# Another order for the opening of a one-core sum of linear attention and a gated product: loads, value projections and first half units

## The chip, the cores and the metric

The kernel runs on one core of a Trainium2 chip. The metric is the device time of one execution in microseconds (us); the median of several executions counts. TensorE (PE) multiplies 128x128 weights with a moving operand and writes to PSUM, of which there are eight banks. ScalarE (ACT) and VectorE (DVE) copy and combine what lies there; GpSimd (POOL) works on SBUF; SyncE (SP) issues the loads.

## The reference, cut to what matters

```python
x = A_x                                   # 1 x 2048 x 512, bf16
xn = _layernorm(x, axis=-1)
# A: linear attention, 32 heads of 16
qkv = (xn @ wqkv)...                      # q, k, v
pq, pk = einsum(q, w_phi), einsum(k, w_phi)
phi = concatenate([softmax(p), softmax(-p)])      # for q and for k
kv = einsum("bhsf,bhsd->bhfd", phi_k, v); z = sum of phi_k over s
o = einsum(phi_q, kv) / (einsum(phi_q, z) + 1e-6)
# B: gated bilinear
g = einsum("bsd,df->bsf", xn, w_gate); u = einsum("bsd,df->bsf", xn, w_up)
return x + o @ wo + (g * u) @ w_down      # F = 1792
```

## The kernel before

The 2048 tokens are 16 tiles (NT) of 128, in groups of four (GT). A tile is normalised with tokens on the partitions (xn, 128x512); the products need it transposed, features on the partitions (xnT, four chunks of 128). For tiles 0 to 3 the transposes are made on TensorE with an identity (lt, line 216): four 128x128 transposes write one PSUM bank (tp), and ScalarE copies it to xnT in two halves of 128x256 (line 223, parts=2). Later tiles are normalised on ScalarE and transposed by DMA (ln_block).

The order of each engine's instructions is the order in which the code issues them (a manual schedule): no planner moves them. Each engine does its own in that order and waits at semaphores, which the build sets by what writes and reads each tile. So the code from line 378 on, the opening, is the schedule:

- first_stats, first_std, first_apply: mean and variance of a tile on VectorE (ln_sums, line 161), the root on ScalarE (line 371), reciprocal and scaling on VectorE (lines 375 and 177).
- warm_up (line 324): matmuls of ones into a bank that nobody reads, nine at the start and one after the transposes of tile 0.
- vproj(n) (line 332 on): the values of tile n, four matmuls of 128x512 (proj, line 252), evicted to vt on ScalarE or VectorE (line 339). For tile 0 the transposes of tile 1 stand between its first two matmuls and the last two, and its eviction is issued later.
- unit(T, f, lo, hi): for a group T of four tiles and a chunk f of 128 hidden features, four gate matmuls and four up matmuls (line 288), the gate copied by ScalarE (g_sb, line 294) and multiplied with up by VectorE (hT, line 297). For f = 0 and 1 of group 0 it is done in halves of 256 tokens, tiles 0 and 1 first; the transposes of tile 2 and 3 stand between gate and up of these half units (amid), and the copies of tile 2 and 3 after the gate's copy.
- then the values of tiles 2 and 3, the table load for exp, the second halves (unit(0, f, 2 * P, TT)), and from there whole units in turn with the folding of w_phi into the k weights (fold, line 243), kproj, kv and so on.

All PSUM tiles but kv come from one pool of six banks in rotation (bank); the two others are kvps, opened ahead of the opening, which accumulate phi_k with v later.

SP's queue has the loads in this order: x of tiles 0 and 1, the two halves of wv, x of tiles 2 and 3, gate and up weights of chunks 0 and 1 (dma_gu, line 78), wphi, gate and up of chunks 2 and 3, and so on.

Of the kernel before, what the change touches and what calls it, by code (L numbers as in the profile page):

```python
# [8 lines left out]
BF16 = mybir.dt.bfloat16  # L9
F32 = mybir.dt.float32  # L10
AF = mybir.ActivationFunctionType
ALU = mybir.AluOpType
# [9 lines left out]
def kernel(  # L22
# [51 lines left out]
    def dma_x(lo, hi):  # L74
        nc.sync.dma_start(out=xall[:, lo:hi, :], in_=x_view(lo, hi))  # L75
# [4 lines left out]
    def dma_gu(lo, hi):  # L80
        dma_cols(nc.sync, wg, B_w_gate, lo * P, hi * P)
        dma_cols(nc.sync, wu, B_w_up, lo * P, hi * P)
# [3 lines left out]
    for lo in (0, 2):  # L86
        nc.sync.dma_start(out=wv[:, lo:lo + 2, :],  # L87
                          in_=A_wqkv[lo * P:(lo + 2) * P, 2 * D:3 * D].rearrange("(c p) f -> p c f", p=P))
    dma_x(2, 3)
    dma_x(3, 4)  # L90
    dma_gu(0, 2)
    nc.sync.dma_start(out=wphi[:], in_=A_w_phi.rearrange("(c h) d f -> (h d) c f", c=DC))
    dma_gu(2, 4)
    nc.sync.dma_start(out=wT2[:, 1, :, :], in_=A_wqkv[:, D:2 * D], transpose=True)
# [59 lines left out]
    def bank(name, dt=F32, n=TT):  # L154
        return ps_s.tile([P, n], dt, name=name, tag="s")
# [3 lines left out]
    def ln_sums(n):  # L159
        stats = lnpool.tile([P, nc.vector.BN_STATS_DIM], F32, name="stats")  # L160
        nc.vector.bn_stats(out=stats[:], in_=xall[:, n, :])  # L161
        return stats
# [12 lines left out]
    def ln_apply(n, mean, rstd):  # L175
        xn = xnpool.tile([P, D], BF16, name="xn")
        nc.vector.tensor_scalar(out=xn[:], in0=xall[:, n, :], scalar1=mean, scalar2=rstd,
                                op0=ALU.subtract, op1=ALU.mult)
        xns[n] = xn

    def mv_tile():
        return lnpool.tile([P, GT, nc.vector.BN_AGGR_DIM], F32, name="mv", bufs=GT)
# [30 lines left out]
        for i in range(GT):  # L213
            chores.append(lambda i=i: apply(i))

    def lt(n, parts=1, later=False):
        tp = bank("tp", BF16).rearrange("p (c t) -> p c t", c=DC)
        for c in range(DC):
            nc.tensor.transpose(out=tp[:, c, :], in_=xns[n][:, c * P:(c + 1) * P], identity=ident[:])

        def copies():
            for c in range(0, DC, DC // parts):
                nc.scalar.copy(out=xnT[:, c:c + DC // parts, n * P:(n + 1) * P], in_=tp[:, c:c + DC // parts, :])  # L223

        if later:
            return copies
        copies()

    bd = consts.tile([P, DC, 8, DH], BF16)

# [19 lines left out]
    def proj(ps, n, w, js=range(DC)):  # L250
        for j in js:
            nc.tensor.matmul(ps, lhsT=xnT[:, j, n * P:(n + 1) * P], rhs=w[:, j, :],  # L252
                             start=(j == 0), stop=(j == DC - 1))
# [24 lines left out]
    hTs = {}  # L278
    units = [(T, f) for T in range(NGRP) for f in range(FC)]

    def unit(T, f, lo=0, hi=TT, amid=None):
        if T not in hTs:
            hTs[T] = hpool.tile([P, FC, TT], BF16, name="hT", tag="h")
        pss = []
        for w, name in ((wg, "g"), (wu, "u")):
            ps = bank(name)[:, 0:hi - lo]
            for c in range(DC):
                nc.tensor.matmul(ps, lhsT=w[:, c, f * P:(f + 1) * P], rhs=xnT[:, c, T * TT + lo:T * TT + hi],  # L288
                                 start=(c == 0), stop=(c == DC - 1))
            pss.append(ps)  # L290
            if amid is not None and name == "g":
                copies = amid()
        g_sb = gpool.tile([P, TT], BF16, name="g_sb")
        nc.scalar.copy(out=g_sb[:, 0:hi - lo], in_=pss[0])  # L294
        if amid is not None:
            copies()
        nc.vector.tensor_tensor(out=hTs[T][:, f, lo:hi], in0=pss[1], in1=g_sb[:, 0:hi - lo], op=ALU.mult)  # L297

    def ffn(k):
        for _ in range(k):  # L300
# [24 lines left out]

    warm_up(9)

    with tc.tile_pool(name="ps_k", bufs=1, space=PSUM) as ps_k:
        kvps = [ps_k.tile([P, 4, 4, E1], F32, name=f"kv{b}") for b in range(2)]
        phiks = {}  # L330

        def vproj(n, copy=nc.scalar.copy, amid=None, later=False):
            ps = bank("pv")
            proj(ps, n, wv, range(2))
            if amid is not None:
                amid()
            proj(ps, n, wv, range(2, DC))
            def evict():
                copy(out=vts[n % NV][:, :, :, 0:DH], in_=ps.rearrange("p (a b c) -> p a b c", a=8, b=4))
            if later:  # L340
                return evict
            evict()

        def kproj(n, pf=None):
            phiks[n] = features(n, W1k, "k", pf)

        def vkproj(n):
            pv, pk = bank("pv"), bank("k")
            for j in range(DC):
                proj(pv, n, wv, (j,))  # L350
                proj(pk, n, W1k, (j,))
            nc.scalar.copy(out=vts[n % NV][:, :, :, 0:DH], in_=pv.rearrange("p (a b c) -> p a b c", a=8, b=4))  # L352
            kproj(n, pk)

        def kv(n):
            vt, phik = vts[n % NV], phiks[n]
            for gr in range(NG):
                nc.tensor.matmul(kvps[gr // 4][:, gr % 4, :, :].rearrange("p a b -> p (a b)"),  # L358
                                 lhsT=phik[:, gr, :], rhs=vt[:, gr, :, :].rearrange("p a b -> p (a b)"),
                                 start=(n == 0 and gr % 4 == 0), stop=(n == NT - 1 and gr % 4 == 3))  # L360

        mvs = [mv_tile() for n in range(GT)]
        stds = {}

        def first_stats(n):
            stats = ln_sums(n)
            nc.vector.bn_aggr(out=mvs[n][:, 0, :], in_=stats[:])

        def first_std(n):
            stds[n] = lnpool.tile([P, 1], F32, name="std", bufs=GT)  # L370
            nc.scalar.activation(out=stds[n][:], in_=mvs[n][:, 0, 1:2], func=AF.Sqrt, bias=epst[:], scale=1.0)

        def first_apply(n):
            rstd = lnpool.tile([P, 1], F32, name="rs1", bufs=GT)
            nc.vector.reciprocal(out=rstd[:], in_=stds[n][:])
            ln_apply(n, mvs[n][:, 0, 0:1], rstd[:])

        first_stats(0)
        first_std(0)
        stats1 = ln_sums(1)  # L380
        first_apply(0)
        nc.vector.bn_aggr(out=mvs[1][:, 0, :], in_=stats1[:])
        first_std(1)
        first_apply(1)
        first_stats(2)
        stats3 = ln_sums(3)
        lt(0, parts=2)
        warm_up(1)
        copy_v = vproj(0, amid=lambda: lt(1, parts=2), later=True)
        first_std(2)  # L390
        first_apply(2)
        copy_v()
        nc.vector.bn_aggr(out=mvs[3][:, 0, :], in_=stats3[:])
        first_std(3)
        first_apply(3)
        make_bd()
        nc.gpsimd.tensor_tensor(out=M4[:], in0=BO[:, 0:4, :], in1=BO[:, 4:8, :], op=ALU.add)
        vproj(1)
        unit(0, 0, 0, 2 * P, amid=lambda: lt(2, parts=2, later=True))
        unit(0, 1, 0, 2 * P, amid=lambda: lt(3, parts=2, later=True))  # L400
        vproj(2, copy=nc.vector.tensor_copy)
        vproj(3, copy=nc.vector.tensor_copy)
        table(AF.Exp, 1)
        for f in range(2):
            unit(0, f, 2 * P, TT)
        del units[0:2]
        ffn(1)
        for j0 in (0, 2):
            fold(1, W1k, j0, (nc.scalar.copy, nc.vector.tensor_copy))
        ffn(1)  # L410
        ln_block(4)
        ffn(1)
        chore(2)
        kproj(0)
        ffn(1)
        chore(2)
        ffn(1)
        chore()
        kproj(1)
        ffn(1)  # L420
        chore()
        ffn(1)
        kproj(2)
        chore()
        ffn(1)
        kv(0)
        chore()
        ffn(1)
        kproj(3)
        chore()  # L430
        ffn(1)
        kv(1)
        nc.sync.dma_start(out=wT2[:, 0, :, :], in_=A_wqkv[:, 0:D], transpose=True)
        for n in range(GT, NT):
            if n in (4, 8):
                ln_block(n + 4)
            vkproj(n)
            chore(1 if n % GT < 2 else 0)
            ffn(1)
            kv(n - 2)  # L440
            chore((1, 2, 2, 2)[n % GT])
            if n >= 8 and n % 2 == 0:
                qproj((n - 8) // 2)
            if n == 6:
                fold(0, W1q, 0)
            ffn(1)
            if n == 6:
                fold(0, W1q, 2)
        ffn(1)
        kv(NT - 2)  # L450
        ffn(1)
        kv(NT - 1)
        for b in range(2):
            nc.vector.tensor_tensor(out=KV[:, 4 * b:4 * b + 4, :, :], in0=kvps[b][:],
                                    in1=_bcast_ap(M4[:], [M4[:].ap[0], [0, 4], [E1, 4], [1, E1]]), op=ALU.mult)
        qproj(4)
        ffn(1)
# [64 lines left out]
```

## Time and profile before

| | |
|---|---|
| Time, three executions | 222.0, 222.24, 222.48 us; median 222.24 |
| Profiled execution | 222.45 us; span of its instructions 220.7 us |
| TensorE's last matmul ends | 217.89 us after the span's start |
| Matmuls in the span | 1284 recorded |

Times in the profile count from the span's start. A row of the timeline merges neighbours of one line on one engine: start, time from the first's start to the last's end, engine, line, operation, what is written and read, and how many. A matmul's duration contains its way through the array, so neighbours overlap; the distance of their starts is what TensorE spends on each. The square brackets give the idle time of the engine before, and what ended it. PEld is the loading of the weights, which overlaps the matmul before it. When the loads land, in us: x of tile 0 at 2.80, of tile 1 at 3.35, wv at 4.58 and 5.33, x of tile 2 at 6.08, of tile 3 at 6.72, gate weights of chunks 0 and 1 at 8.35, up weights of these at 9.32, wphi at 9.58.

The opening on VectorE, for tiles 2 and 3:

```profile
6.11 0.69 DVE L161 BATCH_NORM_STATS2 stats<-xall 128x6 f32<-128x512 bf16 x1 [0.22 <-DMA xall<-in_A_x_dram]
8.05 0.16 DVE L375 RECIPROCAL rs<-std 128x1 f32<-128x1 f32 x1 [0.45 <-ACT std L371]
8.25 0.41 DVE L177 TENSOR_SCALAR xn<-xall,mv,rs 128x512 bf16<-128x512 bf16 x1
9.12 0.16 DVE L375 RECIPROCAL rs<-std 128x1 f32<-128x1 f32 x1 [0.36 <-ACT std L371]
```

### The profile page before, as it was taken

The numbers are of one execution on the slowest core, as the hardware profiler recorded it, in microseconds if no ns is written. First come the engines' busy times: TensorE is split into PE (matmuls) and PEld (weight loads), VectorE is DVE, ScalarE is ACT, GpSimd is POOL, SyncE is SP. The second block draws the span as 40 slices with busy tenths as digits, with TensorE's granted clock in tenths as the row PEclk, the third lists the DMA queues.
The fourth block names the chain that finished last, engine by engine and source line by source line (L and its number), as shares of the span: only waits on it lengthen the run. The fifth ranks groups of instructions, "written<-read, shape, count | busy, mean of one in ns | idle before, by whom it ended". The sixth has DMA issues, their size and how long they took to land.

```text
span 220.7 us, 3490 instructions
## 1 busy us (share of the span) xinstructions
PE 215.6 (98%) x1284; PEld 104.8 (47%) x1308; DVE 138.7 (63%) x241; ACT 89.5 (41%) x170; POOL 68.8 (31%) x54
## 2 busy tenths in 40 slices
PE   8999999999999999999999999999999999999994
PEld 2554444445444444444544444444444444454443
DVE  4657985785569685757589964197645745454321
ACT  3755575449764875545353221231322323100000
POOL 3000455545335653637333643033033033000000
PEclk9999999999999999999999999999999999999999
DMA  5999983503200324020206645214431431422401
GB/s 182 237 310 386 367 217 69 97 0 48 31 18 12 57 43 81 9 42 1 49 1 96 119 97 109 62 24 95 95 74 24 95 71 28 91 52 71 71 27 48
DMA packets 47249, 19.91 MB, mean 90 GB/s; under 512 B 37504, under 2 KB 46976, under 8 KB 47104
## 3 DMA queue, kind: packets, MB, share of 16 engines
q1 hardware_dynamic: 47232, 19.69, 38.2%
q8 instruction: 10, 0.16, 0.3%
q14 instruction: 7, 0.06, 0.1%
HBM read 8.67 MB, written 2.10 MB: 49 GB/s over the span
## 4 chain that ended last, share of the span: by engine, by line
PE 94%; DMA 2%; SPq 1%; issue 1%; ACT 0%; DVE 0%
PE u L288 22%; PE fin L310 22%; PE g L288 21%; PE fin L313 6%; PE k L252 6%; PE q L252 6%; PE pv L252 5%; DMA wu<-in_B_w_up_dram 2%; PE ab L465 2%; PE kv L358 2%; SPq L75 1%; PE pq L243 1%; SPq L87 0%; SPq L78 0%; ACT g_sb L294 0%
## 5 line engine op out<-in xcount | busy, mean ns | idle before, releaser
L288 PE MATMUL u<-xnT,wu 128*128 128x512 bf16 (+1 forms) x229 | 57.7, 372 | 0.4
L288 PE MATMUL g<-xnT,wg 128*128 128x512 bf16 (+1 forms) x222 | 56.7, 372 | 0.4
L297 DVE TENSOR_TENSOR hT<-u,g_sb 128x512 bf16<-128x512 f32 (+1 forms) x58 | 37.3, 649 | 26.3 <-PE u L288 16.9
L265 DVE TENSOR_REDUCE sums<-e 128x64 f32<-128x1024 f32 x32 | 38.9, 1216 | 21.8 <-ACT e L262 21.8
L294 ACT CAST g_sb<-g 128x512 bf16<-128x512 f32 (+1 forms) x58 | 33.4, 576 | 45.9 <-PE g L288 45.7
L310 PE MATMUL fin<-wd,hT 128*128 128x512 bf16 (+2 forms) x234 | 50.9, 366 | 0.3
L269 POOL TENSOR_TENSOR phiq<-e,rs 128x1024 bf16<-128x1024 f32 x16 | 30.9, 1932 | 60.8 <-DVE rs L267 53.6
L269 POOL TENSOR_TENSOR phik<-e,rs 128x1024 bf16<-128x1024 f32 x16 | 30.9, 1932 | 55.5 <-DVE rs L267 44.0
L288 PEld LDWEIGHTS <-wu 128*128 128x128 bf16 x232 | 22.6, 98 | 25.8 <-DMA wu<-in_B_w_up_dram 0.2
L310 PEld LDWEIGHTS <-hT 128*128 128x128 bf16 x238 | 22.4, 98 | 24.7
L288 PEld LDWEIGHTS <-wg 128*128 128x128 bf16 x232 | 21.9, 98 | 23.4 <-DMA wg<-in_B_w_gate_dram 0.2
L252 PEld LDWEIGHTS <-xnT 128*128 128x128 bf16 x192 | 17.4, 98 | 18.7 <-ACT xnT L223 1.3
L316 DVE TENSOR_TENSOR o_sb<-fin,xall 128x512 bf16<-128x512 f32 (+2 forms) x17 | 11.2, 657 | 22.3 <-PE fin L313 22.2
L252 PE MATMUL pv<-wv,xnT 128*128 128x512 bf16 x62 | 22.1, 386 | 0.1
L252 PE MATMUL k<-W1k,xnT 128*128 128x512 bf16 x63 | 21.9, 379 | 0.1
L261 ACT ACTIVATE e<-q 128x512 f32<-128x512 f32 x16 | 9.5, 596 | 25.4 <-PE q L252 20.0
L267 DVE RECIPROCAL rs<-sums 128x64 f32<-128x64 f32 x32 | 17.7, 553 | 3.1
L313 PE MATMUL fin<-wo,oT 128*128 128x512 bf16 (+2 forms) x68 | 16.6, 367 | 0.0
L252 PE MATMUL q<-W1q,xnT 128*128 128x512 bf16 x60 | 15.9, 378 | 0.1
L352 ACT CAST vt<-pv 128x512 bf16<-128x512 f32 x12 | 7.0, 587 | 17.4 <-PE pv L252 17.4
L161 DVE BATCH_NORM_STATS2 stats<-xall 128x6 f32<-128x512 bf16 x16 | 10.7, 667 | 1.4 <-DMA xall<-in_A_x_dram 1.4
L474 DVE TENSOR_TENSOR otok<-ab,rden 128x512 bf16<-128x512 f32 x16 | 11.1, 691 | 0.6
(51 smaller groups left out, 118.6 us busy)
## 6 DMA issues: line engine op xcount, KB each, us to landing
out_dram<-o_sb SPq DMA_DIRECT2D x15, 128.0 KB, 2.0
wd<-in_B_w_down_dram SPq DMA_DIRECT2D x1, 1792.0 KB, 15.9
wg<-in_B_w_gate_dram SPq DMA_DIRECT2D x2, 640.0 KB, 6.8
wu<-in_B_w_up_dram SPq DMA_DIRECT2D x2, 640.0 KB, 8.0
xall<-in_A_x_dram SPq DMA_DIRECT2D x1, 1024.0 KB, 11.9
xall<-in_A_x_dram SPq DMA_DIRECT2D x4, 128.0 KB, 2.7
wv<-in_A_wqkv_dram SPq DMA_DIRECT2D x2, 256.0 KB, 3.0
wg<-in_B_w_gate_dram SPq DMA_DIRECT2D x2, 256.0 KB, 4.8
```

The lines of the kernel that those rows point to most:

```text
L161: nc.vector.bn_stats(out=stats[:], in_=xall[:, n, :])
L252: nc.tensor.matmul(ps, lhsT=xnT[:, j, n * P:(n + 1) * P], rhs=w[:, j, :], start=(j == 0), stop=(j == DC - 1))
L265: nc.vector.tensor_reduce(out=sums[:], in_=ev, axis=AX.X, op=ALU.add)
L267: nc.vector.reciprocal(out=rs[:].rearrange("p a b -> p (a b)"), in_=sums[:])
L269: nc.gpsimd.tensor_tensor(out=phi[:].rearrange("p g (x f) -> p (g x) f", f=DH), in0=ev, in1=rs[:].to_broadcast((P, 2 * H, DH)), op=ALU.mult)
L288: nc.tensor.matmul(ps, lhsT=w[:, c, f * P:(f + 1) * P], rhs=xnT[:, c, T * TT + lo:T * TT + hi], start=(c == 0), stop=(c == DC - 1))
L294: nc.scalar.copy(out=g_sb[:, 0:hi - lo], in_=pss[0])
L297: nc.vector.tensor_tensor(out=hTs[T][:, f, lo:hi], in0=pss[1], in1=g_sb[:, 0:hi - lo], op=ALU.mult)
L310: nc.tensor.matmul(ps, lhsT=hTs[T][:, f, t4 * P:(t4 + 1) * P], rhs=wd[:, f, lo:lo + w], start=(f == 0), stop=False)
L313: nc.tensor.matmul(ps, lhsT=oTs[n][:, c, :], rhs=wo[:, c, lo:lo + w], start=False, stop=(c == DC - 1))
L316: nc.vector.tensor_tensor(out=o_sb[:], in0=ps, in1=xall[:, n, lo:lo + w], op=ALU.add)
L474: nc.vector.tensor_tensor(out=o_tok[:].rearrange("p (b h d) -> p b h d", b=2, d=DH), in0=abv[:, :, :, 0:DH], in1=rden[:].to_broadcast((P, ...
```

## The change

Two loads change places: the gate weights of chunks 0 and 1 come before x of tile 3, the up weights after it. lt now issues two transposes, the copy of these, two transposes, the copy of these; in the built program the third transpose of each tile carries a wait for that first copy. unit is split into half (four matmuls), gate_copy and hidden, which the opening calls one by one. The opening has a new order: after the values of tiles 0 and 1 come the gate of half unit 0, the transposes of tile 2, the gate of half unit 1, the values of tile 2, both ups, the transposes of tile 3 and its values. The values of tiles 0 and 1 lie in two PSUM banks of their own (ps_v), which are given back before kvps takes them. Statistics of tiles 2 and 3 are taken one after the other, each with its scaling; make_bd moves to the opening's end; the copies of the values are a function of their own (vcopy). What follows the table load is as before.

```diff
--- before.py
+++ after.py
@@ -87,8 +87,9 @@
         nc.sync.dma_start(out=wv[:, lo:lo + 2, :],
                           in_=A_wqkv[lo * P:(lo + 2) * P, 2 * D:3 * D].rearrange("(c p) f -> p c f", p=P))
     dma_x(2, 3)
+    dma_cols(nc.sync, wg, B_w_gate, 0, 2 * P)
     dma_x(3, 4)
-    dma_gu(0, 2)
+    dma_cols(nc.sync, wu, B_w_up, 0, 2 * P)
     nc.sync.dma_start(out=wphi[:], in_=A_w_phi.rearrange("(c h) d f -> (h d) c f", c=DC))
     dma_gu(2, 4)
     nc.sync.dma_start(out=wT2[:, 1, :, :], in_=A_wqkv[:, D:2 * D], transpose=True)
@@ -213,18 +214,13 @@
         for i in range(GT):
             chores.append(lambda i=i: apply(i))
 
-    def lt(n, parts=1, later=False):
+    def lt(n, parts=2):
         tp = bank("tp", BF16).rearrange("p (c t) -> p c t", c=DC)
-        for c in range(DC):
-            nc.tensor.transpose(out=tp[:, c, :], in_=xns[n][:, c * P:(c + 1) * P], identity=ident[:])
-
-        def copies():
-            for c in range(0, DC, DC // parts):
-                nc.scalar.copy(out=xnT[:, c:c + DC // parts, n * P:(n + 1) * P], in_=tp[:, c:c + DC // parts, :])
-
-        if later:
-            return copies
-        copies()
+        step = DC // parts
+        for lo in range(0, DC, step):
+            for c in range(lo, lo + step):
+                nc.tensor.transpose(out=tp[:, c, :], in_=xns[n][:, c * P:(c + 1) * P], identity=ident[:])
+            nc.scalar.copy(out=xnT[:, lo:lo + step, n * P:(n + 1) * P], in_=tp[:, lo:lo + step, :])
 
     bd = consts.tile([P, DC, 8, DH], BF16)
 
@@ -278,23 +274,27 @@
     hTs = {}
     units = [(T, f) for T in range(NGRP) for f in range(FC)]
 
-    def unit(T, f, lo=0, hi=TT, amid=None):
+    def half(w, name, T, f, lo, hi):
+        ps = bank(name)[:, 0:hi - lo]
+        for c in range(DC):
+            nc.tensor.matmul(ps, lhsT=w[:, c, f * P:(f + 1) * P], rhs=xnT[:, c, T * TT + lo:T * TT + hi],
+                             start=(c == 0), stop=(c == DC - 1))
+        return ps
+
+    def gate_copy(ps, n):
+        g_sb = gpool.tile([P, TT], BF16, name="g_sb")
+        nc.scalar.copy(out=g_sb[:, 0:n], in_=ps)
+        return g_sb
+
+    def hidden(T, f, ps, g_sb, lo, hi):
         if T not in hTs:
             hTs[T] = hpool.tile([P, FC, TT], BF16, name="hT", tag="h")
-        pss = []
-        for w, name in ((wg, "g"), (wu, "u")):
-            ps = bank(name)[:, 0:hi - lo]
-            for c in range(DC):
-                nc.tensor.matmul(ps, lhsT=w[:, c, f * P:(f + 1) * P], rhs=xnT[:, c, T * TT + lo:T * TT + hi],
-                                 start=(c == 0), stop=(c == DC - 1))
-            pss.append(ps)
-            if amid is not None and name == "g":
-                copies = amid()
-        g_sb = gpool.tile([P, TT], BF16, name="g_sb")
-        nc.scalar.copy(out=g_sb[:, 0:hi - lo], in_=pss[0])
-        if amid is not None:
-            copies()
-        nc.vector.tensor_tensor(out=hTs[T][:, f, lo:hi], in0=pss[1], in1=g_sb[:, 0:hi - lo], op=ALU.mult)
+        nc.vector.tensor_tensor(out=hTs[T][:, f, lo:hi], in0=ps, in1=g_sb[:, 0:hi - lo], op=ALU.mult)
+
+    def unit(T, f, lo=0, hi=TT):
+        pg = half(wg, "g", T, f, lo, hi)
+        pu = half(wu, "u", T, f, lo, hi)
+        hidden(T, f, pu, gate_copy(pg, hi - lo), lo, hi)
 
     def ffn(k):
         for _ in range(k):
@@ -325,21 +325,65 @@
 
     warm_up(9)
 
+    def vcopy(n, ps, copy=nc.scalar.copy):
+        copy(out=vts[n % NV][:, :, :, 0:DH], in_=ps.rearrange("p (a b c) -> p a b c", a=8, b=4))
+
+    mvs = [mv_tile() for n in range(GT)]
+    stds = {}
+
+    def first_std(n, stats):
+        nc.vector.bn_aggr(out=mvs[n][:, 0, :], in_=stats[:])
+        stds[n] = lnpool.tile([P, 1], F32, name="std", bufs=GT)
+        nc.scalar.activation(out=stds[n][:], in_=mvs[n][:, 0, 1:2], func=AF.Sqrt, bias=epst[:], scale=1.0)
+
+    def first_apply(n):
+        rstd = lnpool.tile([P, 1], F32, name="rs1", bufs=GT)
+        nc.vector.reciprocal(out=rstd[:], in_=stds[n][:])
+        ln_apply(n, mvs[n][:, 0, 0:1], rstd[:])
+
+    with tc.tile_pool(name="ps_v", bufs=1, space=PSUM) as ps_v:
+        pv = [ps_v.tile([P, D], F32, name=f"pv{n}") for n in range(2)]
+        first_std(0, ln_sums(0))
+        stats = ln_sums(1)
+        first_apply(0)
+        first_std(1, stats)
+        first_apply(1)
+        lt(0)
+        warm_up(1)
+        proj(pv[0][:], 0, wv, range(2))
+        lt(1)
+        proj(pv[0][:], 0, wv, range(2, DC))
+        proj(pv[1][:], 1, wv)
+        first_std(2, ln_sums(2))
+        first_apply(2)
+        vcopy(0, pv[0])
+        g = [half(wg, "g", 0, 0, 0, 2 * P)]
+        lt(2)
+        g.append(half(wg, "g", 0, 1, 0, 2 * P))
+        pv2 = bank("pv")
+        proj(pv2, 2, wv)
+        stats = ln_sums(3)
+        g_sb = [gate_copy(g[0], 2 * P)]
+        first_std(3, stats)
+        first_apply(3)
+        g_sb.append(gate_copy(g[1], 2 * P))
+        vcopy(1, pv[1])
+        u0 = half(wu, "u", 0, 0, 0, 2 * P)
+        hidden(0, 0, u0, g_sb[0], 0, 2 * P)
+        vcopy(2, pv2, nc.vector.tensor_copy)
+        u1 = half(wu, "u", 0, 1, 0, 2 * P)
+        hidden(0, 1, u1, g_sb[1], 0, 2 * P)
+        lt(3)
+        pv3 = bank("pv")
+        proj(pv3, 3, wv)
+        make_bd()
+        vcopy(3, pv3, nc.vector.tensor_copy)
+        table(AF.Exp, 1)
+        nc.gpsimd.tensor_tensor(out=M4[:], in0=BO[:, 0:4, :], in1=BO[:, 4:8, :], op=ALU.add)
+
     with tc.tile_pool(name="ps_k", bufs=1, space=PSUM) as ps_k:
         kvps = [ps_k.tile([P, 4, 4, E1], F32, name=f"kv{b}") for b in range(2)]
         phiks = {}
-
-        def vproj(n, copy=nc.scalar.copy, amid=None, later=False):
-            ps = bank("pv")
-            proj(ps, n, wv, range(2))
-            if amid is not None:
-                amid()
-            proj(ps, n, wv, range(2, DC))
-            def evict():
-                copy(out=vts[n % NV][:, :, :, 0:DH], in_=ps.rearrange("p (a b c) -> p a b c", a=8, b=4))
-            if later:
-                return evict
-            evict()
 
         def kproj(n, pf=None):
             phiks[n] = features(n, W1k, "k", pf)
@@ -349,7 +393,7 @@
             for j in range(DC):
                 proj(pv, n, wv, (j,))
                 proj(pk, n, W1k, (j,))
-            nc.scalar.copy(out=vts[n % NV][:, :, :, 0:DH], in_=pv.rearrange("p (a b c) -> p a b c", a=8, b=4))
+            vcopy(n, pv)
             kproj(n, pk)
 
         def kv(n):
@@ -359,48 +403,6 @@
                                  lhsT=phik[:, gr, :], rhs=vt[:, gr, :, :].rearrange("p a b -> p (a b)"),
                                  start=(n == 0 and gr % 4 == 0), stop=(n == NT - 1 and gr % 4 == 3))
 
-        mvs = [mv_tile() for n in range(GT)]
-        stds = {}
-
-        def first_stats(n):
-            stats = ln_sums(n)
-            nc.vector.bn_aggr(out=mvs[n][:, 0, :], in_=stats[:])
-
-        def first_std(n):
-            stds[n] = lnpool.tile([P, 1], F32, name="std", bufs=GT)
-            nc.scalar.activation(out=stds[n][:], in_=mvs[n][:, 0, 1:2], func=AF.Sqrt, bias=epst[:], scale=1.0)
-
-        def first_apply(n):
-            rstd = lnpool.tile([P, 1], F32, name="rs1", bufs=GT)
-            nc.vector.reciprocal(out=rstd[:], in_=stds[n][:])
-            ln_apply(n, mvs[n][:, 0, 0:1], rstd[:])
-
-        first_stats(0)
-        first_std(0)
-        stats1 = ln_sums(1)
-        first_apply(0)
-        nc.vector.bn_aggr(out=mvs[1][:, 0, :], in_=stats1[:])
-        first_std(1)
-        first_apply(1)
-        first_stats(2)
-        stats3 = ln_sums(3)
-        lt(0, parts=2)
-        warm_up(1)
-        copy_v = vproj(0, amid=lambda: lt(1, parts=2), later=True)
-        first_std(2)
-        first_apply(2)
-        copy_v()
-        nc.vector.bn_aggr(out=mvs[3][:, 0, :], in_=stats3[:])
-        first_std(3)
-        first_apply(3)
-        make_bd()
-        nc.gpsimd.tensor_tensor(out=M4[:], in0=BO[:, 0:4, :], in1=BO[:, 4:8, :], op=ALU.add)
-        vproj(1)
-        unit(0, 0, 0, 2 * P, amid=lambda: lt(2, parts=2, later=True))
-        unit(0, 1, 0, 2 * P, amid=lambda: lt(3, parts=2, later=True))
-        vproj(2, copy=nc.vector.tensor_copy)
-        vproj(3, copy=nc.vector.tensor_copy)
-        table(AF.Exp, 1)
         for f in range(2):
             unit(0, f, 2 * P, TT)
         del units[0:2]
```

## The prediction

> **What bounds the kernel now.** I read the page first. TensorE is busy over nearly the whole span, and the chain of work that ended last is TensorE's matmuls:
>
> ```profile
> PE 215.6 (98%) x1284; PEld 104.8 (47%) x1308; DVE 138.7 (63%) x241; ACT 89.5 (41%) x170; POOL 68.8 (31%) x54
> PE 94%; DMA 2%; SPq 1%; issue 1%; ACT 0%; DVE 0%
> ```
>
> So a microsecond that TensorE loses or wins anywhere in its stream moves the end by as much, unless it waits later for something timed by a DMA. The busy times of the stretches say that it hardly does: from 12.6 us on TensorE (the first figure after the stretch's length) is busy 204.09 of 208.10 us, of which 2.8 us lie after its last matmul (217.89 us), and the view of waits shows in that stretch no weight load that waits for a DMA.
>
> ```profile
> 12.60:220.70 208.10, 204.09 (x1228) 99.31 (x1249) 131.10 (x215) 81.78 (x152) 66.96 (x44) 1.00 0.36 83
> ```
>
> The change lies before 12.6 us. So the third view is TensorE's timeline there (start, duration, line, how many). Tile n's four transposes are a tp row:
>
> ```profile
> 4.88 0.61 PE L219 MATMUL tp<-ident,xn 128*128 128x128 bf16 x4
> 5.28 0.63 PE L324 MATMUL warm<-const-bfloat16-1.0 128*128 128x512 bf16 x1
> 5.95 0.97 PE L252 MATMUL pv<-wv,xnT 128*128 128x512 bf16 x2
> 6.75 0.39 PE L219 MATMUL tp<-ident,xn 128*128 128x128 bf16 x4
> 6.98 1.66 PE L252 MATMUL pv<-wv,xnT 128*128 128x512 bf16 x6
> 8.48 0.60 PE L288 MATMUL g<-xnT,wg 128*128 128x256 bf16 x4
> 8.92 0.39 PE L219 MATMUL tp<-ident,xn 128*128 128x128 bf16 x4
> 9.37 0.61 PE L288 MATMUL u<-xnT,wu 128*128 128x256 bf16 x4
> 11.13 1.67 PE L252 MATMUL pv<-wv,xnT 128*128 128x512 bf16 x7
> ```
>
> and the waits, with ScalarE's copies of the transposes:
>
> ```profile
> PEld L252 <- ACT xnT L223: 1.3, 3, 0.6
> PEld L288 <- DMA wu<-in_B_w_up_dram: 0.2, 1, 0.2
> ```
>
> ```profile
> 5.52 0.65 ACT L223 COPY xnT<-tp 128x256 bf16<-128x256 bf16 x2 [0.28 <-PE tp L219]
> 7.18 0.65 ACT L223 COPY xnT<-tp 128x256 bf16<-128x256 bf16 x2 [1.01 <-PE tp L219]
> ```
>
> What to see. In single instructions the four transposes of tile 1 start at 6.75, 6.81, 6.87 and 6.92, the first copy of them at 7.18, its release comes at 7.56, and the matmul that needs it starts at 7.605: **0.683 us from a transpose's start, over ScalarE, back to TensorE** (0.256 + 0.381 + 0.046). For tile 0 it is 5.17 to 5.95, 0.778, as TensorE runs at half pace: 128x512 matmuls follow one another by 0.427 us until 6.7 and by 0.216 after (the granted clock reads 1.00 throughout, since its record begins at 6.72; the pitch tells more). TensorE's idle time here is 0.245 ahead of pv at 5.95 and 0.195 ahead of 7.605 (both for that copy), and 0.23 ahead of 9.37 (up weights, landed 9.32): 0.67 in all, and the change can win no more than that.
>
> **The change part by part.** TensorE does the same 16 transposes, 16 v matmuls and 16 half-width gate and up matmuls; only order and waits differ.
>
> *Transposes in two halves.* This decides. Before, four transposes of a tile ran, then two copies. Now it is two, copy, two, copy, into one PSUM bank, and in the built program the third transpose of each tile carries a wait for the copy of the first two. TensorE takes matmuls in order, so everything behind waits too. Price, by the hand-over above: the third starts 0.683 after the second instead of one pitch (0.056), so 0.627 for tiles 1, 2 and 3 each: **+1.88**. Bounds for one: 0.56, if a matmul whose weights are loaded already starts on the release with nothing of the 0.046 and a bit less in ScalarE; 0.70 from ScalarE's longest such copy (0.394). For tile 0 the second starts at 4.96, its copy at 4.96 + 0.35 = 5.31, the release is at 5.69, the third at 5.73, the fourth at 5.84, the filler matmul at 5.95 and the first pv at 6.38. It was 5.95: **+0.43**. The old 0.245 is inside that.
>
> Weighed against a rule: the Trainium skill (PSUM — Partial Sum Buffer, section on PSUM bank collisions) says that TensorE must not write a bank while ScalarE reads it, so accesses are to be guarded by bank, not by address; without the guard the sum would be 221.6, with it 224.1. No run here shows the collision; the wait stands in the program.
>
> *Clock.* The two pv ahead of tile 1's transposes took 5.95 to 6.75, mostly at half pace. From 6.38 they take 0.34 at half pace, 0.04 for the rest of the first and 0.22 for the second, to 6.98, if the pace rises at 6.72 as before: 0.60 instead of 0.80, **-0.20**.
>
> *Waits that go.* pv of tile 1 begins after four 0.216 matmuls, when its copies are long released (8.41 for the second, wanted at 8.69): **-0.195**. The up matmuls come after pv of tile 2, at 11.70, 2.4 us after their weights landed: **-0.23**.
>
> *A wait that comes.* pv of tile 3 stands right behind its transposes. The third of these starts at 13.32, the fourth at 13.37, the second copy is usable at 13.37 + 0.683 = 14.06; pv's first two end at 13.86: **+0.20**. For tile 2 a gate half of 0.44 lies between and covers it.
>
> *Loads.* SP's queue gives wg before the fourth x tile; no issue is added, wu and all behind keep their place. wg lands by 8.35 (as before, or earlier) and is wanted at 9.12. x of tile 3 may slip from 6.72 to wg's 8.35; VectorE is busy with tile 2 until 9.24, so this costs nothing; without that cover it would delay tile 3's transposes, which have 0.47 to spare (next).
>
> *Normalisation later.* The square root of tile 2 queues on ScalarE behind tile 1's second copy (8.03), so 8.29, released 8.61; tile 2 is usable 0.65 later (by 8.026 to 8.67 before) at 9.26; its transposes come at 9.56. Tile 3's waits behind tile 2's second copy (10.61) and a gate copy (0.27): 11.15, usable 12.11, wanted 12.58. Both nothing, with 0.30 and 0.47 of cover.
>
> *The rest.* v of tiles 0 and 1 in banks of their own frees two of the rotating six; those banks pass to kv, whose first matmul comes past 30 us. Copies of v wait behind others, but nobody reads them before that. ScalarE's table load (1.28) slides to 13.9, and the first gate copy of the second halves starts some 0.3 late; its bank is wanted again 2 us later. bd is ready by 14.3, the fold comes at 18. Nothing.
>
> Sum: 0.43 + 1.88 - 0.20 - 0.195 - 0.23 + 0.20 = **+1.88 us**: the gate of the second halves starts at 14.5 instead of 12.64. The profiled execution took 222.45 (span 220.7 and 1.7 around it), 0.2 over the median of 222.24; it becomes 224.3, and the median **224.1**.
>
> **The rivals.**
>
> *The clock rises late* (225.3). At the old rise, 6.72, TensorE had idled 0.245 since 5.28; now it idles 0.67 from 5.06 on, and the pace may stay half. For: the first 5.9 us of nearly unbroken filler were needed. Against: in those 5.9 us there were gaps too. From 6.98 to 14.5 there are 5.46 us of matmuls at full pace and 2.08 of waits, so 72% work; at half pace 1 us of the stretch lasts 1.72, and each us spent so loses 0.72 / 1.72 = 0.42. Bounds: a rise later by the new idle time alone (0.67) costs 0.67 x 0.42 = 0.28; one counted anew for 5.9 us from 5.73, at 11.6, costs 4.9 x 0.42 = 2.05. The middle is 1.2. The Trainium skill (TensorE: Matmul & The Clock Gate, Part 1) has a free-running window of 3.41 us that must be busy; one window more gives 10.13, +1.43 and 225.5. Its "around 4 us" of activity isn't what this trace shows (5.9).
>
> *Not slower* (221.6): TensorE goes on past a waiting transpose with matmuls that are ready, and only the 0.67 of idle time is won. It decides once four hand-overs cost under 0.17 each. Against: at 9.14 TensorE idled 0.23 for the up weights while the next gate half was ready (its weights landed at 8.35), and didn't take it first.
>
> *Cheaper hand-overs* (223.2): the first two transposes' copy overlaps more than the trace shows, or an early clock (rise at 4.3 instead of 6.72 would save the 0.43 of half pace ahead and some hand-over, 0.6 in all). Both together leave +1.0.
>
> That the change doesn't do what it says is excluded by the built program's order.
>
> **How the numbers follow.** Forecast 0.60 (own range 223.4 to 224.7: four hand-overs by ±0.07, the clock by -0.4 to +0.3); late clock 0.30; cheaper hand-overs 0.05; not slower 0.05. The range takes in two thirds of the late clock: 223.4 to 225.7, leaving out below 2 in 10. A measurement of this kernel can tell about 0.2% (0.45 us). Slower: 0.60 + 0.30 + 0.05 = 0.95, of which I move 0.01 to same for the edge of the third; the not-slower case gives faster 0.03 and same 0.02.
>
> **What would show it.** Right: between the second and third transpose of each tile about 0.68 us (0.78 for tile 0) in which a copy of 128x256 lies; pv at 6.4; no wait for up weights; the second halves' gate at 14.5; TensorE's busy time from there on unchanged. Wrong: third transposes a pitch behind the second; pitches of 0.427 past 7 us (the clock); a wait for a DMA or for VectorE's xn ahead of tile 2's or 3's transposes; or a gap beyond 15 us in TensorE that takes the delay up.

## The result, and the profile after

Median 224.63 us (six executions), before 222.2 (six): 2.4 us slower, ratio 1.0109 with a 95% interval of 1.0069 to 1.015. The six lie in two groups: 223.77, 223.83, 223.91 and 225.35, 225.49, 225.81; the median is the middle of the gap between them. The profiled execution is of the second: 225.49, span 223.7. Its page has the busy times and the chain as before, with TensorE (PE) nearly all of it:

```profile
PE 216.8 (97%) x1284; PEld 105.3 (47%) x1308; DVE 138.6 (62%) x241; ACT 89.9 (40%) x170; POOL 68.9 (31%) x54
PE 95%; DVE 1%; DMA 1%; issue 1%; ACT 1%
```

The busy times from the second halves' gate on (15.64 us, before at 12.64; stretch, its length, then TensorE's busy time):

```profile
15.64:223.70 208.06, 204.04 (x1228) 99.30 (x1249) 131.03 (x214) 82.39 (x152) 66.97 (x44) 1.00 0.35 77
```

204.04 of 208.06 us, before 204.09 of 208.10: nothing was won or lost after the opening. All of it, 15.64 - 12.64 = 3.00 us, came ahead of that point. TensorE's timeline there:

```profile
4.96 0.39 PE L222 MATMUL tp<-ident,xn 128*128 128x128 bf16 x2
5.81 0.37 PE L222 MATMUL tp<-ident,xn 128*128 128x128 bf16 x2 [0.46 <-ACT xnT L223]
5.98 0.63 PE L324 MATMUL warm<-const-bfloat16-1.0 128*128 128x512 bf16 x1
6.41 1.06 PE L248 MATMUL pv<-wv,xnT 128*128 128x512 bf16 x2
7.26 0.42 PE L222 MATMUL tp<-ident,xn 128*128 128x128 bf16 x2
8.14 0.37 PE L222 MATMUL tp<-ident,xn 128*128 128x128 bf16 x2 [0.46 <-ACT xnT L223]
8.30 2.13 PE L248 MATMUL pv<-wv,xnT 128*128 128x512 bf16 x6
10.27 0.60 PE L280 MATMUL g<-xnT,wg 128*128 128x256 bf16 x4
10.71 0.28 PE L222 MATMUL tp<-ident,xn 128*128 128x128 bf16 x2
11.44 0.27 PE L222 MATMUL tp<-ident,xn 128*128 128x128 bf16 x2 [0.46 <-ACT xnT L223]
12.85 1.04 PE L280 MATMUL u<-xnT,wu 128*128 128x256 bf16 x8
14.46 0.27 PE L222 MATMUL tp<-ident,xn 128*128 128x128 bf16 x2 [0.46 <-ACT xnT L223]
14.79 1.02 PE L248 MATMUL pv<-wv,xnT 128*128 128x512 bf16 x3
15.64 0.60 PE L280 MATMUL g<-xnT,wg 128*128 128x256 bf16 x4
```

and the waits, where a line that the kernel before did not have stands for the third transposes:

```profile
PE tp L222 <- ACT xnT L223: 1.8, 4, 0.5
PEld L248 <- ACT xnT L223: 0.5, 1, 0.5
```

Two things are to be seen. Each tp row of before is now two rows, 0.73 to 0.88 us apart, and the second is each time released by ScalarE's copy. (The bracket shows 0.46, since a matmul's recorded duration runs on; in starts the third transpose comes 0.773 after the second for tiles 0 and 1, and 0.679 and 0.678 for tiles 2 and 3.) And six pv matmuls take 8.30 to 10.27, where in the kernel before six take 1.5 us, 0.2 of it a wait: their starts are 0.427 apart up to 9.65 us and 0.216 after. The record of the granted clock begins at 9.65 here, and at 6.72 in the profile before. The pace rose nearly a whole 3 us later.

### The profile page after: what moved, and what is told of

It reads as the page before. It is cut to its first block, busy times and chain, and to the rows that moved or that the text cites. A ratio compares the mean times of both kernels' runs of the same rounds, so it can differ in the third digit from the quotient of the medians.

```text
span 223.7 us, 3489 instructions
## 1 busy us (share of the span) xinstructions
PE 216.8 (97%) x1284; PEld 105.3 (47%) x1308; DVE 138.6 (62%) x241; ACT 89.9 (40%) x170; POOL 68.9 (31%) x54
## 4 chain that ended last, share of the span: by engine, by line
PE 95%; DVE 1%; DMA 1%; issue 1%; ACT 1%
PE u L280 22%; PE fin L310 22%; PE g L280 21%; PE pv L248 7%; PE fin L313 6%; PE k L248 6%; PE q L248 6%; PE ab L467 2%; PE kv L402 2%; PE tp L222 1%; DMA xall<-in_A_x_dram 1%; ACT xnT L223 1%; PE pq L239 1%; DVE stats L162 1%; PE warm L324 0%
## 5 line engine op out<-in xcount | busy, mean ns | idle before, releaser
L248 PE MATMUL pv<-wv,xnT 128*128 128x512 bf16 x62 | 23.0, 401 | 0.1
L329 ACT CAST vt<-pv 128x512 bf16<-128x512 f32 x14 | 8.2, 589 | 17.7 <-PE pv L248 17.6
```

## The experiments

My theory after this: the waits for the copy in the shared bank cost 1.3 to 1.9 us by themselves, and their idle time keeps the clock at half pace for longer in some executions (the late group, against the early one), which costs about 1.5 us more. The rivals: the new order or the loads cost it; splitting a step into halves costs it; the late clock is chance.

**Transposes together again.** The changed kernel with lt as it was: four transposes, then two copies.

```diff
-        for lo in range(0, DC, step):
-            for c in range(lo, lo + step):
-                nc.tensor.transpose(out=tp[:, c, :], ...)
-            nc.scalar.copy(out=xnT[:, lo:lo + step, ...], in_=tp[:, lo:lo + step, :])
+        for c in range(DC):
+            nc.tensor.transpose(out=tp[:, c, :], ...)
+        for lo in range(0, DC, step):
+            nc.scalar.copy(out=xnT[:, lo:lo + step, ...], in_=tp[:, lo:lo + step, :])
```

> The changed kernel, but a tile's four transposes run before both copies again. Theory (the waits of the third transposes cost the time): the four hand-overs go, 1.88 + 0.43 us. What stays of waits by the 0.683 hand-over: 0.195 ahead of tile 1's values, 0.683 - 0.056 - 0.436 = 0.19 ahead of tile 2's, 0.63 ahead of tile 3's, against 0.195 + 0.23 in the kernel before: at most +0.6, less with an early clock, so 222.1 to 222.9, and no execution over 223.5. Rival (the new order or the moved loads cost the time): stays at 223.5 or more.

Measured: 222.81 (222.64 to 223.21), ratio to the kernel before 1.0027 (1.0015 to 1.0038). One group; the median lies in the range, three of seven are above it by up to 0.3, none over 223.5. 1.8 of the 2.4 us go with the split. In its profile TensorE idles 0.196, 0.190 and 0.626 ahead of the values of tiles 1, 2 and 3, as reckoned.

**Two banks.** The split stays, but each half has a PSUM bank of its own.

```diff
     def lt(n, parts=2):
-        tp = bank("tp", BF16).rearrange("p (c t) -> p c t", c=DC)
         step = DC // parts
         for lo in range(0, DC, step):
+            tp = bank("tp", BF16).rearrange("p (c t) -> p c t", c=DC)
```

> The changed kernel with the two halves of a tile's transposes in two PSUM banks, so still two transposes, copy, two transposes, copy, but without the shared bank. Theory (it is the wait for the bank, not the splitting): no wait at the third transpose, and the first copy starts two transposes earlier than in the kernel before; the waits for the up weights and most of those for copies are gone: 221.6 to 222.5, no execution over 223. Rival (smaller steps between TensorE and ScalarE cost by themselves): 223.5 or more.

Measured: 222.54 (222.19 to 222.94), ratio 1.0011 (1.0002 to 1.0019). The median is 0.04 above the range, six of eleven executions lie above it, and none is over 223. So it is not the splitting: with the wait for the bank gone, the four transposes follow one another again. The timeline of TensorE:

```profile
10.02 1.04 PE L280 MATMUL u<-xnT,wu 128*128 128x256 bf16 x8
10.89 0.39 PE L222 MATMUL tp<-ident,xn 128*128 128x128 bf16 x4
11.63 1.04 PE L248 MATMUL pv<-wv,xnT 128*128 128x512 bf16 x4 [0.35 <-ACT xnT L223]
```

Three waits of TensorE are there that the kernel before did not have. The largest is that of tile 3's values, which stand right behind their transposes: in starts the idle time is 11.634 - 11.118 = 0.52. The others are 0.10 us for the gate weights, which land at 7.92, and 0.08 ahead of tile 2's values, so the expectation that the waits were gone held only in part.

**A filler in the wait.** The changed kernel with a matmul of ones between the second and third transpose, in tiles 0 and 1, and in another kernel in all four tiles.

```diff
             nc.scalar.copy(out=xnT[:, lo:lo + step, ...], in_=tp[:, lo:lo + step, :])
+            if n < 2 and lo == 0:      # the other kernel: if lo == 0
+                nc.tensor.matmul(warm, lhsT=ones[:, 0:P], rhs=ones, start=True, stop=True)
```

> The changed kernel with one filler matmul of ones (0.427 us at half pace, 0.216 at full) in the wait between second and third transpose of tiles 0 and 1. It fits into the idle 0.67, so every hand-over stays. Theory (idle time in the opening keeps the clock back in some executions): TensorE is busier before the clock's decision, it rises by 7 us, and all executions lie at 223.4 to 224.2, none near 225.4. Rival (when the clock rises is chance and has nothing to do with these waits): about half of the executions stay at 225.3 to 225.8.

Measured: 223.89 (four executions, 223.88 to 224.09), ratio 1.0075 (1.0062 to 1.0088).

> The changed kernel with the filler matmul in the wait of all four tiles. Theory: the fillers of tiles 2 and 3 (0.216 at full pace in 0.63 of idle time) change nothing, those of tiles 0 and 1 bring the clock early: all executions at 223.7 to 224.2, none near 225.4. Rival (the four executions with fillers in two tiles were early by chance): some at 225.3 or more.

Measured: 223.92 (five, 223.77 to 224.26, the last a little above the range), ratio 1.0068 (1.0056 to 1.008). In both the hand-over stays (in the first, tile 1's pairs at 6.55 and 7.28, tile 2's at 9.12 and 9.86) and the late group is gone: none of nine, against 7 of 12 in the changed kernel and the one with old loads. The added work made the kernel faster in its median. This rests on the times alone: in the two profiled executions the record of the clock begins at 3.55 and 3.99, before the first filler in a wait (5.17 and 5.07), so that these two show an early clock but not what a filler does to it.

**Old loads.** The changed kernel with x of tile 3 ahead of the gate weights again.

```diff
     dma_x(2, 3)
-    dma_cols(nc.sync, wg, B_w_gate, 0, 2 * P)
     dma_x(3, 4)
-    dma_cols(nc.sync, wu, B_w_up, 0, 2 * P)
+    dma_gu(0, 2)
```

> The changed kernel with the loads in the old order (x of tile 3 before the gate weights). Theory (the loads have cover on both sides): nothing changes; executions at 223.8 and at 225.4 as in the changed kernel. Rival (the moved loads cost or win time): differs from the changed kernel's 223.8 group by more than 0.3.

Measured: 223.74, 223.91, 225.3, 225.48, 225.65, 225.65; ratio 1.0131 (1.0107 to 1.0156). The same two groups: the loads play no part in the changed kernel's time, and the higher median only counts four late clocks instead of three. Its profiled execution (223.74) is of the early group, with the record of the clock from 4.91, and shows what the waits alone do:

```profile
6.42 0.27 PE L221 MATMUL tp<-ident,xn 128*128 128x128 bf16 x2
7.15 0.27 PE L221 MATMUL tp<-ident,xn 128*128 128x128 bf16 x2 [0.46 <-ACT xnT L222]
7.26 1.46 PE L247 MATMUL pv<-wv,xnT 128*128 128x512 bf16 x6
13.92 0.60 PE L279 MATMUL g<-xnT,wg 128*128 128x256 bf16 x4
```

The second halves' gate starts at 13.92, 1.28 later than before, and the execution took 1.29 longer than the profiled one before (222.45).

**The split alone.** The kernel before in its old order, with the copies in between the transposes of tiles 0 and 1 only.

```diff
+        if not later:
+            step = DC // parts
+            for lo in range(0, DC, step):
+                for c in range(lo, lo + step):
+                    nc.tensor.transpose(out=tp[:, c, :], ...)
+                nc.scalar.copy(out=xnT[:, lo:lo + step, ...], in_=tp[:, lo:lo + step, :])
+            return
```

> The kernel before, in its old order, with nothing changed but the copies of tiles 0 and 1, which now come in between their transposes (two, copy, two, copy, one bank). Theory (waits for the bank, and a late clock by their idle time): the two hand-overs add 0.43 + 0.63, less 0.195 and less the 0.23 that TensorE waits for the up weights anyway and what an earlier clock gives back: +0 to +0.5 where the clock rises early (222.2 to 222.7), and +1.4 to +1.9 where it rises a window late (223.6 to 224.1), some executions of each. Rival (the waits alone, no clock): one group at 222.2 to 222.9.

Measured: six executions at 222.31 to 222.41 and six at 223.97 to 224.32, two of these a little over the range; ratio 1.0036 (1.0013 to 1.0058); before 222.43 in the same runs. The early group lies at the time of the kernel before, so two hand-overs cost nothing there. The expectation gave the wait for the up weights and an earlier clock as the reason; no profile of that group was taken, so this is not shown. The late group is 1.7 above, without any other change. The profiled execution (224.05) is of it. Its timeline has the two waits, and six pv after them, whose starts are 0.427 apart up to 9.68 us and 0.22 after:

```profile
5.90 0.37 PE L222 MATMUL tp<-ident,xn 128*128 128x128 bf16 x2 [0.46 <-ACT xnT L223]
8.23 0.37 PE L222 MATMUL tp<-ident,xn 128*128 128x128 bf16 x2 [0.46 <-ACT xnT L223]
8.39 2.10 PE L259 MATMUL pv<-wv,xnT 128*128 128x512 bf16 x6
```

**Less filler at the start.** The kernel before with four matmuls of ones instead of nine.

```diff
-    warm_up(9)
+    warm_up(4)
```

> The kernel before with four filler matmuls at the start instead of nine, so that TensorE idles from 2.5 us to 4.88, where it waited for nothing else; no wait is added, no other instruction changes. Theory (idle time ahead keeps the clock at half pace a window longer): all executions slower and spread, +0.1 to +1.8, so 222.3 to 224.0, median about 223.2. Rival (the clock rises some fixed time after the first matmul, whatever the idle time): 222.0 to 222.7 as before.

Measured: 223.54 (five, 223.32 to 223.97), ratio 1.0047 (1.0034 to 1.006). Taking away work that nothing waits for costs 1.1 us. The record of the clock begins at 10.58; in the timeline the idle time, and the six pv at half pace:

```profile
0.82 1.87 PE L324 MATMUL warm<-const-bfloat16-1.0 128*128 128x512 bf16 x4 [0.82 <-PEq L506]
4.94 0.61 PE L219 MATMUL tp<-ident,xn 128*128 128x128 bf16 x4 [2.25 <-DVE xn L177]
7.27 2.77 PE L252 MATMUL pv<-wv,xnT 128*128 128x512 bf16 x6
```

**Tile 3's transposes earlier.** The two-banks kernel with lt(3) between the two up halves.

```diff
+        lt(3)
         u1 = half(wu, "u", 0, 1, 0, 2 * P)
         hidden(0, 1, u1, g_sb[1], 0, 2 * P)
-        lt(3)
```

> As the kernel with two banks for the halves, and tile 3's transposes stand between the two up halves instead of behind them, so that 0.44 us of up matmuls cover most of the 0.51 us that tile 3's values waited for the copy. Theory (what is left over the kernel before is that wait): 222.54 - 0.4 = 222.1, 221.7 to 222.4. Rival (the rest is the loads, which land later than the faster order wants them): 222.4 to 222.6 as with two banks.

Measured: 222.11 (221.75 to 222.37), ratio 0.9987 (0.9978 to 0.9995): 0.13% (0.3 us) below the kernel before, whose executions in the same runs (222.07 to 222.70) overlap with these, and the lowest median of all the runs. In its timeline tile 3's values follow the up half with 0.08 of idle time in place of 0.52:

```profile
10.74 0.40 PE L222 MATMUL tp<-ident,xn 128*128 128x128 bf16 x4
10.98 0.60 PE L280 MATMUL u<-xnT,wu 128*128 128x256 bf16 x4
11.49 1.04 PE L248 MATMUL pv<-wv,xnT 128*128 128x512 bf16 x4
```

## Why the prediction was right, and where not

Slower was right, and the measured median lies in the range; the forecast's size, +1.88, is between the two groups (+1.6 and +3.3), and its own condition, a clock that rises by 6.7 us, held in half of the executions only, as far as their times tell. That the median came 0.5 from the forecast is in part luck: it is the middle of three early and three late executions, none lies within 0.7 of it, and with four late ones, as with the old loads, it is 225.4.

- *Transposes in two halves*: right in place and price. 0.679 and 0.678 were measured for tiles 2 and 3 against 0.683; 0.773 for tile 0 against 0.778. For tile 1 it was 0.773, not 0.683, as the pace was still half. Two banks in place of one show that the wait is for the bank, by the semaphore that the build sets there: the split itself costs nothing.
- *Clock*: the step that failed. The prediction took one time of the rise for the kernel, early or late; the executions show both. It put -0.20 for two pv that would run partly at full pace from 6.72. In the profiled execution the pace rose at 9.65. Tile 1's transposes began at 7.26 instead of 6.98, its hand-over was 0.09 longer, and pv ran at half pace to 9.65: the gate came at 10.27 instead of 9.12. That is 1.15, and 14.5 + 1.15 is 15.65; it came at 15.64. So the whole difference between forecast and this execution is the clock, and the pitches of 0.427 past 7 us are the sign that the prediction had named for it. Its price for the late clock, 0.42 for each us, would be 1.23 for the 2.94 us. The other group was not profiled in the changed kernel; by the old-loads profile, with a rise at 4.91, the sum is +1.28, which is the 1.88 less the 0.6 that I had put for an early clock. So the second halves' gate came at 13.92 or 15.64, and in neither profile at the forecast 14.5.
- *The late clock as a rival*: 225.3 was forecast, 225.35 to 225.81 measured. The chance of 0.30 was low: 3 of 6, with the old loads 4 of 6, with the split alone 6 of 12. That idle time of TensorE causes it is shown from both sides in the times, by the fillers (none of nine late) and by less filler (all five slower, with a rise at 10.58 in the one profiled).
- *Waits that go, the wait that comes*: no weight load waits for the up weights; tile 3's values waited 0.195 ahead of their third matmul (15.196 - 15.00), forecast 0.20.
- *Loads, normalisation, the rest*: nothing, as forecast; the old loads changed nothing and the time from the second halves on is the same within 0.05. This holds behind the hand-overs only: with two banks and tile 3's transposes earlier, TensorE idles 0.16 and 0.08 us for the normalised x of tiles 2 and 3.
- *Not slower* and *cheaper hand-overs* fell: the third transposes held everything behind them, at the full price. Of the second, the early clock came in half of the executions. Of the 0.67 that the first counted, 0.27 is there once the bank is not shared and tile 3's transposes stand in a better place: the second halves' gate then comes at 12.37 instead of 12.64.

## What to carry to other kernels

A step may be halved to let the next engine start early, but if both halves lie in one PSUM bank, a guard by bank, as this build sets it, makes the writer wait for the reader between them: here 0.68 us from start to start at full pace and 0.77 at half, against 0.056 and 0.107 unsplit. Give each half its own bank, or do not split. And in an opening, price a wait of TensorE twice: by its length, and by what the later clock takes from the work behind it; a filler matmul in the wait cost nothing measurable here (223.9, as the early group), and with it no execution was late.

## What the runs showed of the hardware

The record of the granted clock is 211.626, 215.04 or 218.453 us long in the nine traces that have one, always a multiple of 3.413 (62, 63, 64). Its start lies at 6.72, 9.65, 5.16, 3.75, 3.55, 4.91, 10.58, 6.06 and 3.99, so its place in steps of 3.413 is not the same each time (the remainders go from 0.14 to 3.30). So the rise comes at the end of such a stretch, whose place against the kernel's start differs from one execution to another. The Trainium skill (TensorE: Matmul & The Clock Gate, Part 1) tells of a free-running window of 3.413 us, which agrees.

How busy the stretch must be can be bounded. Before, the pace rose at 6.72; TensorE idled 0.51 of the 3.41 us ahead of it (0.26 before the first transposes, 0.245 before pv), so it was busy for 85%; the stretch ahead of that, idle for its first 0.93 us (0.11 ahead of the span and 0.82 in it), had 73% and did not bring it. In the changed kernel the stretch to 6.24 had 0.34 and 0.67 of idle time, 70%, and did not bring it; the one to 9.65 had 0.67, 80%, and did. The bound lies between 73% and 80% by these. The seven other records fit: the stretch that ends at the rise is busy for 80% or more, the one ahead of it for 58% at most. That a share is what counts was not tested by itself. By this bound, a filler of 0.427 in the second of the two gaps would lift the changed kernel's stretch to 6.24 from 70% to 83%, which fits that no execution with fillers was late; this is an estimate from the changed kernel's trace.

Why the kernel before is always near 222.2, though its clock should also rise at different times, is not shown, as there is one trace of it. It would fit its wait for the up weights at 9.3, since what an early rise wins ahead of that wait is lost in it. The changed order has taken that cover away.
